# Batch 0's q of two head groups as whole rows, w_in in other pieces, four column pairs of the first batch by halves, transposes also on PSUM pairs, and a new hand-written order

## The chip, the cores and the metric

The kernel runs on one core of one Trainium2 chip. The metric is the time of one execution in device microseconds (us); the figure for a kernel is the median of its runs. The engines are called as the profile calls them: PE (matrix multiply, with PEld for the weight loads beside it), ACT and DVE (element by element), POOL and SP (here they mostly issue transfers).

## The reference, cut to what matters

```python
# q, k, v: (8 batches, 12 heads, 448 rows, 64); w_in: (768, 2048); w_out: (2048, 768)
scores = (q @ k.transpose) / 8
attn   = max(scores, 0)**2 / 448
x      = (attn @ v), heads side by side  -> (8*448 rows, 768)
h      = x @ w_in
out    = gelu_exact(h) @ w_out           # float32, 3584 x 768
```

There is no softmax, so the attention is: scores, relu, square, times v.

## The kernel before, in words

**Work of one batch.** A batch has three groups of four heads. First k and q are turned so that the 64 values of a head lie on partitions (`add_tk` L612 and `add_tq` L639 by PE for batches 0 and 1, tile `tp`, copied out to `kT` and `qT`; by DMA for later batches, `add_T_dma` L667). A step of `add_steps` (L734) multiplies a block of k with q into PSUM (tile `ps`, L752, array split into 64x64 parts), takes relu with the scale (tile `a_sq`; L769 on ACT or L771 on DVE) and squares it (L781 on DVE or L779 on ACT). `add_av` (L814) multiplies seven blocks of squares with v (tile `pav`, L831) and copies the result to `xT` (L519 on DVE, L521 on ACT). Batch 0's steps are done by halves of the 448 rows (`halves` L1468), so a step's q part is 224 wide. All other products use the whole 128x128 array: `x @ w_in` (plain: `add_f1` L880, tile `psh`, L891, gelu L901; or as 2x2 blocks with seven products instead of eight: `add_early` L989 and `add_unit` L1036, tile `pe`, L1048; for the last batch `add_block` L1188, tile `pb`, L1199) and `h @ w_out` (`add_group` L1339, tile `pso`, L1375, summed to `osb` by L1409, stored by L1328). The seven-product form needs sums of weights (`ws`, L962, and `t_sb`, L1309) and of activations (`t_x`, L1007, and `s_sb`, L1356), all on DVE.

**The beginning.** Batch 0's first head group is loaded by the ACT and SP queues as float32 (`k32`, `q32`) and cast by ACT and DVE (`early` L1528); everything else is loaded by POOL, cast on the way. Until data come, PE runs nine products of zeros (`spin`, L1510), and `Z` entries of the order put in further ones (`fill`, L1677). Batch 0's q is loaded by halves of its rows: `add_q(0, g, g + 1, 0, HC)` for groups 1 and 2, and one load `add_q(0, 0, G, HC, NC)` for the second half of all three groups. w_in comes in five pieces of columns of 128 (`WINS` L37, `add_win` L592, three DMAs each), w_out in five DMAs (`add_wout` L599). Six of batch 0's sixteen columns of `x @ w_in` are done plainly by halves of the rows (`HALF_M` L53: pairs starting at 0, 8, 10; 12 matmuls of 224 for a pair and half), columns 2 and 3 plainly for all rows (12 matmuls of 448), the rest by seven products.

**What sets the order.** A recorded list of operations is placed by `ORDER` (L83): each word is an engine (P and Q for PE, A for ACT, D for DVE, G for POOL, S for SP) and the number of an operation; `place` (L360) issues them in that order. Each engine's instructions run in that order, and an instruction that waits holds up all behind it on its engine. A `Q` calls the operation's `split` (L799 for steps, `add_av` has one too): the step then takes two single PSUM banks of `f_pp` (two in all) instead of one pair of banks of `w_pp` (three in all). The planner's durations in the tuples decide nothing at run time where `ORDER` names the operation, and `ORDER` names all.

Of the kernel before, what the change touches and what calls it, by code (L numbers as in the profile page):

```python
# [8 lines left out]
F32 = mybir.dt.float32  # L9
# [4 lines left out]
KC = 112  # L14
NC = S // KC
# [21 lines left out]
WINS = ((0, 2), (6, 8), (8, 12), (2, 6), (12, 16))  # L37
# [15 lines left out]
HALF_M = (0, 8, 10)  # L53
# [30 lines left out]
G0 G1616 G1 G3 G4 G7 D13 Z1024 A10 G118 A16 G2 P14 D15 P11 D12 P17 D18 P19 D20 P42 A43 P36 A37 P33  # L84
P21 D44 D22 P23 A24 D34 P51 P25 A52 D26 P48 Q39 D35 G117 P54 A49 D40 P63 A64 D55 P57 P27 D28 P29 D30
P69 P66 A58 D59 P31 D32 A70 D71 A67 G121 G6 G125 D38 P90 P93 D41 A94 D65 P131 A132 P102 A103 P129
P45 A46 A47 G126 Z672 A91 P84 D130 Q159 D50 D68 P72 G5 A160 D85 G8 G122 A73 G120 P111 A112 A53 D56
D74 P75 P133 D76 P156 D113 A157 A134 P81 D82 P139 A140 P60 D61 D83 P96 P108 D62 A97 D109 P137 P78
A79 D86 D80 P174 A175 D77 D92 P135 A136 D95 G124 P171 A172 D104 D98 P87 A88 P105 D89 A106 P168 A169
P141 A142 P162 D107 D110 D138 P195 A163 P99 D100 Q114 G119 P207 D101 D176 P165 A196 A115 D116 A158  # L90
P198 A199 D173 P143 A144 D208 D170 A166 D197 P240 A241 A161 D250 D251 P180 D181 D167 G128 G123 G9
D164 P222 A223 P192 P242 A243 P244 D253 D209 P145 A193 A146 P213 A214 A245 D194 P177 A178 D200 P189
A179 P183 D215 D190 D191 P246 A184 A247 P210 D182 A211 P216 P186 A187 D185 P248 A249 P258 P275 A217
D254 G127 G236 D188 P219 A276 G235 G238 G147 A220 Q201 D224 D212 D255 G148 P204 A202 A203 A205 D252
A221 P260 P277 A206 D259 P261 P278 A262 D409 D280 D218 D257 P265 D256 P282 A283 A266 Q225 A279 D412
D263 P270 P267 A226 A227 D371 D372 P284 D268 A269 P287 D285 P375 A264 A281 P392 A393 P273 G150 D271
P290 D288 P382 P399 D447 D374 A376 P378 P395 A274 D373 D450 A289 A291 D448 G151 P377 D451 P394 D397
A286 A400 A383 P387 P404 D380 A396 A379 P384 A272 D405 A406 P401 D388 P413 P430 A389 A414 A431 D385
A386 P420 P437 A421 D402 S228 A438 P407 D452 P390 D410 P416 A391 D411 P433 A408 D455 P442 S229 D454
A417 A434 P415 A398 G153 G154 P432 D443 A444 D435 A436 D418 P422 P439 A403 Q299 A300 P314 A315 P425  # L100
D423 P428 D456 D426 P459 A427 A424 D440 G234 A419 P311 P317 P445 P461 A441 D453 D449 D457 A318 D460
S230 S231 P463 P323 D312 A429 A381 A446 A313 D462 S232 P308 D316 S233 D301 A324 D309 D464 P350 P465
D466 A351 D352 P305 P302 A306 D310 P335 A307 P467 G237 G149 G152 G155 D458 D336 D468 A303 D304 P469
D470 P326 A327 P365 A366 P341 A342 D319 P471 P338 G239 G292 A339 A340 P320 D491 D472 A321 P332 A322
D337 D492 D343 G293 G294 D493 A333 P329 G295 D330 D367 S475 S476 P495 G296 A496 P497 P353 D498 P359
D334 D360 A331 A354 P362 A363 P499 S473 A500 P501 P356 P347 D325 A364 D328 P344 A357 A358 D355 D348
G297 D361 D345 D346 D349 G481 P511 A512 P520 A521 P503 P517 D502 A518 P526 P368 A369 D527 A519 P514
D504 S477 S478 G484 D494 S479 S480 P529 P505 D370 D583 P587 A513 P604 P507 D584 D515 G298 P594 A530
G487 A588 P589 A595 D605 D586 D522 A528 P607 P590 D508 D585 D592 P611 A516 P606 D608 A591 G482 G483
D621 D609 P599 A612 G485 G486 P596 S657 D531 P613 G488 D600 A601 S658 G489 S510 P623 P640 G663 D597  # L110
D614 P616 D617 A610 A641 A624 D622 P602 D506 P619 P625 P642 A593 A615 A603 A620 A598 Q523 D628 D645
A524 A646 P535 P626 P643 D525 S509 A536 A627 P630 P647 P538 A539 D631 D644 Q532 D533 A618 A534 P571
A572 P632 D648 P649 D673 P635 Q550 P553 A554 P652 D650 A651 D633 P638 P655 A656 D551 D674 A639 D636
A637 P677 P577 D653 A654 P559 A560 P547 S659 P679 D552 D675 P565 D548 S660 A678 D680 A578 A555 D540
P562 D563 D537 A566 S661 A567 D676 P681 P683 A682 D684 A634 P541 P574 P544 A545 D546 A629 A564 G666
P685 D686 S474 D542 D543 D693 D694 G490 P687 D688 S691 P689 D690 P568 A575 A549 A569 P556 D695 P719
A557 A558 A720 P713 D714 P697 D698 P725 A726 A727 A576 P728 D729 P722 D696 A570 P699 S692 D700 P731
P737 D732 P701 D702 D723 P703 P705 P746 D579 S662 G669 G664 G665 A561 D573 A747 P580 G667 A581 D704
D706 D730 D582 D785 P716 P709 A717 D710 S712 G668 G670 D786 P789 D788 G671 P806 A724 D790 P791 D794
D807 A738 P796 P813 D814 P707 A718 D787 A733 D715 P808 A739 D811 D708 A721 A812 P809 P792 D823 A810  # L120
P749 A750 Q734 D793 P740 A741 A795 D797 P798 P815 D816 P818 D819 D799 A742 A735 A736 D748 P825 P842
A843 P801 P821 P804 A751 A805 Q770 D802 P752 S711 A822 D826 P828 P845 A846 P832 D824 D753 D829 P849
D875 P827 S859 S860 S861 P844 D754 A850 P854 A800 S862 P834 P851 A771 A803 P879 D855 D830 D852 A833
D835 D847 P837 A817 A820 A853 P840 P857 P764 D876 D838 P755 D765 D877 A880 P883 A756 D878 A836 A858
A831 P773 A774 P761 D762 P881 D882 A841 G865 G868 A848 A884 P743 A763 A839 P767 D768 P918 D766 A775
P885 D886 P887 G672 D757 D888 A744 A856 A919 D745 P889 D890 D772 S893 P933 A934 D895 A935 P758 A759
D896 P779 A780 P776 A777 S863 A760 P891 P899 A900 S864 D898 P945 P927 D892 A778 P921 A922 A928 D946
D781 A947 P903 D920 P901 D897 P942 P948 A949 D769 D943 P782 A783 P924 G871 D902 A904 P930 D929 D931
D932 A925 P905 D906 A784 P907 D908 G866 P951 P915 D923 P939 D987 P909 G867 A940 D926 G869 G870 G872
D910 D988 P911 D912 S914 A952 P991 P1008 A916 A917 D990 Q963 D964 D944 P957 G873 A953 S1061 A958  # L130
D959 P936 A937 Q954 A938 P998 P1015 D992 P993 P1010 D1009 S1062 D989 A999 D950 P1011 A1016 A955
D1013 A1014 A956 P994 D996 P1003 D1012 A995 P1020 P1027 D1025 P1044 P1000 D1021 A1022 D1004 D1028
A1045 D1001 P1029 A997 P1046 D1049 A1050 D1032 A1005 P1030 P1047 D1026 P1017 D1018 A1031 P1034 P1051
D1048 S1063 S1064 S1065 A1002 P1023 P1036 P1053 D1052 D1054 A1035 D1037 P1039 P1056 P1006 G1067
A1007 G1070 D1057 D1079 A1024 P1042 P1059 A1060 P1081 D1040 S913 P978 A1041 A1043 A1058 P1117 D941
A979 P960 A961 D1077 D1078 D1118 P1150 D1151 S894 D962 P1120 P1083 A1121 P966 P972 A1082 P969 A973
P1085 P1141 D980 D967 D1084 A970 D1086 A968 D974 D1080 P981 A982 G874 A1055 P975 P1087 D1088 D1142
P1089 A1033 D1090 A976 P1091 A983 A1019 D1092 A1038 P1144 P1132 D1097 D977 P1147 A965 D971 A1133
A1148 D1134 P1093 P1101 D1094 S1095 S1066 P1129 A1130 P984 A1119 P1126 D1099 D1098 P1103 A985 A986
D1102 P1105 D1104 D1127 A1106 A1145 P1107 P1135 A1131 P1123 P1156 A1124 D1122 P1109 D1143 P1195  # L140
G1073 G1068 A1125 D1136 A1157 P1193 D1189 P1212 G1069 G1071 G1072 D1137 A1149 S1263 P1210 D1108
D1110 P1111 D1100 P1113 G1074 D1128 A1211 D1215 P1165 A1194 G1075 D1198 D1112 S1115 A1199 A1166
A1167 D1114 P1138 D1190 D1192 S1264 S1265 Q1153 S1096 P1200 P1217 P1196 P1213 A1139 A1154 D1140
# [262 lines left out]
def kernel(  # L406
# [169 lines left out]
    def add_v(b, g0, g1):  # L576
# [6 lines left out]
        for g in range(g0, g1):  # L583
            ld_v[b, g] = [o]
# [1130 lines left out]
```

## Time and profile before

| | |
|---|---|
| runs | 360.16, 361.66, 361.63 us; median 361.63 |
| profiled execution: span from first to last instruction | 358.5 us |
| what lies around the span, median less span | 3.1 us |
| PE, PEld busy | 350.0 us (98%), 248.0 us (69%) |
| DVE, ACT, POOL busy | 305.6 us (85%), 270.3 us (75%), 102.9 us (29%) |
| first transpose of PE | at 5.93 us |
| first plain product of `x @ w_in` (`psh`) | at 28.03 us |
| first product of the seven-product form (`pe`) | at 43.90 us |
| first product with w_out (`pso`) | at 71.57 us |
| last matmul ends | at 354.85 us |

Times within the profile are from the span's start. Matmuls overlap, so the busy time of PE counts some waiting as work; the distance between starts is the better measure, and the chain of waits and the timeline give it.

### The profile page before, as it was taken

Reading aid. Unit: us, or ns where it says so; the run is one execution under the profiler, and the core shown is the slowest. Engines: PE = TensorE matmul, PEld = TensorE weight load, DVE = VectorE, ACT = ScalarE, POOL = GpSimd, SP = SyncE. Lnnn points to the kernel's source line nnn. Section 1 sums busy time; section 2 is a strip of 40 time slices with the busy share of each in tenths; the row PEclk is TensorE's granted clock in tenths of the full one; section 3 lists DMA queues with packets and bytes.
Section 4 is the critical chain, followed back from the end, with each engine's and each line's share of the span. In section 5 each row is a group of like instructions: output and inputs, shape, how many; then the busy total and the mean of one; then the engine's idle time right before and its main releaser. Section 6 shows DMA issues by size and latency. Waiting matters only on the chain.

```text
span 358.5 us, 9223 instructions
## 1 busy us (share of the span) xinstructions
PE 350.0 (98%) x3841; PEld 248.0 (69%) x3841; DVE 305.6 (85%) x515; ACT 270.3 (75%) x437; POOL 102.9 (29%) x138
## 2 busy tenths in 40 slices
PE   8879999999999999999999999999999999999995
PEld 3557679955588655896557965579668855788663
DVE  2999999999997989988889898779988998595762
ACT  3999997899869896978978669789986778334300
POOL 8664816096193104700075100841000000000000
PEclk9999999999999999999999999999999999999999
DMA  9999999999999958995399941998402001012222
GB/s 171 197 201 204 201 204 157 146 145 148 183 141 146 214 84 127 154 169 79 63 90 159 214 69 51 88 171 209 72 3 90 2 0 46 3 44 90 88 87 91
DMA packets 124361, 43.01 MB, mean 120 GB/s; under 512 B 102688, under 2 KB 120992, under 8 KB 124320
## 3 DMA queue, kind: packets, MB, share of 16 engines
q0 software_dynamic: 85328, 22.47, 66.2%
q1 hardware_dynamic: 38448, 19.50, 26.0%
q8 instruction: 30, 0.49, 0.5%
q10 hardware_dynamic: 544, 0.46, 0.4%
q14 instruction: 11, 0.09, 0.1%
HBM read 45.61 MB, written 11.01 MB: 158 GB/s over the span
## 4 chain that ended last, share of the span: by engine, by line
PE 92%; ACT 5%; DVE 2%; issue 0%; DVEq 0%; ACTq 0%
PE pso L1375 37%; PE pe L1048 30%; PE ps L752 9%; PE pav L831 8%; PE pb L1199 4%; ACT a_sq L769 3%; PE psh L891 2%; PE spin L1510 1%; DVE a_sq L781 1%; DVE a_sq L771 1%; ACT xT L521 0%; PE tp L620 0%; PE fill L1677 0%; ACT a_sq L779 0%; ACT qT L521 0%
## 5 line engine op out<-in xcount | busy, mean ns | idle before, releaser
L769 ACT ACTIVATE a_sq<-ps 128x896 bf16<-128x896 f32 (+1 forms) x125 | 106.7, 893 | 14.5 <-PE ps L752 14.2
L781 DVE TENSOR_TENSOR a_sq<-a_sq 128x896 bf16<-128x896 bf16 (+1 forms) x108 | 63.8, 615 | 2.1 <-ACT a_sq L769 1.9
L1375 PEld LDWEIGHTS <-s_sb 128*128 128x128 bf16 x456 | 42.4, 98 | 32.3 <-issue 7.1
L1048 PEld LDWEIGHTS <-win_sb 128*128 128x128 bf16 x624 | 59.5, 98 | 2.7 <-issue 1.5
L771 DVE TENSOR_SCALAR a_sq<-ps 128x896 bf16<-128x896 f32 (+1 forms) x57 | 55.5, 988 | 2.6 <-PE ps L752 2.2
L779 ACT ACTIVATE a_sq<-a_sq 128x896 bf16<-128x896 bf16 x61 | 57.2, 959 | 0.5
L752 PE MATMUL ps<-qT,kT 64*64 64x448 bf16 (+1 forms) x756 | 49.7, 337 | 2.7 <-ACT a_sq L769 1.3
L1098 ACT ACTIVATE h_sb<-part 128x448 bf16<-128x448 f32 x78 | 43.2, 580 | 9.9 <-DVE part L1086 9.7
L1086 DVE TENSOR_TENSOR part<-pe,part 128x448 f32<-128x448 f32 x78 | 45.5, 620 | 5.3 <-PE pe L1048 3.6
L1375 PEld LDWEIGHTS <-h_sb 128*128 128x128 bf16 x336 | 31.9, 98 | 22.9 <-issue 4.0
L1048 PEld LDWEIGHTS <-ws 128*128 128x128 bf16 x468 | 44.1, 98 | 3.5 <-issue 2.9
L1375 PE MATMUL pso<-wout_sb,s_sb 128*128 128x384 bf16 (+2 forms) x232 | 41.1, 321 | 0.0
L1375 PE MATMUL pso<-t_sb,s_sb 128*128 128x384 bf16 x224 | 41.1, 327 | 0.0
L1375 PE MATMUL pso<-wout_sb,h_sb 128*128 128x384 bf16 x224 | 41.1, 327 | 0.0
L559 POOL DMA_DIRECT2D nk<-in_k_dram x36 | 34.7, 968 | 9.6 <-DMA wout_sb<-in_moe_w_out_dram 8.1
L831 PE MATMUL pav<-a_sq,v_sb 64*64 64x448 bf16 (+1 forms) x756 | 36.5, 329 | 0.8 <-DVE a_sq L781 0.8
L752 PEld LDWEIGHTS <-kT 64*64 64x64 bf16 x756 | 19.6, 105 | 23.7 <-issue 17.7
L1048 PE MATMUL pe<-t_x,win_sb 128*128 128x224 bf16 x312 | 34.5, 259 | 0.0
L1048 PE MATMUL pe<-xT,win_sb 128*128 128x224 bf16 x312 | 34.1, 259 | 0.0
L1048 PE MATMUL pe<-t_x,ws 128*128 128x224 bf16 x312 | 33.2, 259 | 0.0
L521 ACT COPY part<-pe 128x448 f32<-128x448 f32 x53 | 26.4, 541 | 8.9 <-PE pe L1048 6.2
L1409 DVE TENSOR_TENSOR osb<-pso,p_sb 128x384 f32<-128x384 f32 x42 | 23.3, 554 | 9.4 <-PE pso L1375 5.9
(74 smaller groups left out, 409.5 us busy)
## 6 DMA issues: line engine op xcount, KB each, us to landing
out_dram<-osb SPq DMA_DIRECT2D x19, 384.0 KB, 2.8
nq<-in_q_dram POOLq DMA_DIRECT2D x38, 112.0 KB, 5.8
nk<-in_k_dram POOLq DMA_DIRECT2D x36, 112.0 KB, 5.8
v_sb<-in_v_dram POOLq DMA_DIRECT2D x5, 672.0 KB, 7.6
v_sb<-in_v_dram POOLq DMA_DIRECT2D x9, 224.0 KB, 8.0
win_sb<-in_moe_w_in_dram POOLq DMA_DIRECT2D x8, 192.0 KB, 9.2
wout_sb<-in_moe_w_out_dram POOLq DMA_DIRECT2D x4, 384.0 KB, 12.7
wout_sb<-in_moe_w_out_dram POOLq DMA_DIRECT2D x1, 1536.0 KB, 15.8
```

The costliest lines, as they stand in the source:

```text
L521: A.copy(dst, src)
L559: nc.gpsimd.dma_start(nk[b][:, g0, :, e], rows[:, e].rearrange("p (i d) -> p i d", d=D))
L752: nc.tensor.matmul(side(ps, e)[64 * j : 64 * j + 64, x * w : x * w + w], kT[r, g, i * 128 + 64 * j : i * 128 + 64 * j + 64], moving, start ...
L769: A.activation(to, x, AF.Relu, scale=c_att)
L771: V.tensor_scalar(to, x, c_att, 0.0, op0=mybir.AluOpType.mult, op1=mybir.AluOpType.max,)
L779: A.activation(ar, ar, AF.Square)
L781: V.tensor_mul(ar, ar, ar)
L831: nc.tensor.matmul(side(pav[0], e)[o2 : o2 + 64, :w], vt[b][r, 2 * g + e, bass.ts(i, D)], box["a2"][r, e, o : o + w], start=(i == 0), stop ...
L1048: nc.tensor.matmul(bank[name][:, y, z * HS : z * HS + HS], w[:, k, bass.ts(mm, 128)], right()[:, k], start=first and k == 0 and z == 0, st ...
L1086: V.tensor_add(get(to), ps(name), get(other))
L1098: A.activation(h_ring()[:, m : m + 2, o + half[c].start : o + half[c].stop], src().rearrange("p (x n) -> p x n", x=2), AF.Gelu,)
L1375: nc.tensor.matmul(box[bank][:, n0:n1], left()[:, kf], right()[:, kf, n0:n1], start=bool(need) and kf == 0, stop=kf == K2 - 1, skip_group_ ...
```

## The change

Loads and pieces: `WINS` becomes (0,2), (8,12), (2,6), (12,16), (6,8). Groups 1 and 2 of batch 0's q are each loaded whole; of the second half of the rows only group 0 remains. The identity matrix that the transposes need is made on POOL ahead of the first load instead of behind it. `HALF_M` gets a fourth pair, 2, and columns 2 and 3 are no longer done for all rows at once; the products are the same in total, as 24 matmuls of 224 instead of 12 of 448. The transposes of `add_tk` and `add_tq` may take a pair of banks of `w_pp` instead of a bank of `f_pp` where the order says `Q`. `add_unit` waits for the pieces of w_in that it reads. `ORDER` is wholly new: all engines' instructions stand in another order, and some copies, relus and squares are on the other of ACT and DVE. The durations in the planner's tuples are changed in many places; since `ORDER` names every operation they move nothing by themselves. The core of the diff:

```diff
-WINS = ((0, 2), (6, 8), (8, 12), (2, 6), (12, 16))
+WINS = ((0, 2), (8, 12), (2, 6), (12, 16), (6, 8))
-HALF_M = (0, 8, 10)
+HALF_M = (0, 8, 10, 2)
 ORDER = """
-G0 G1616 G1 G3 G4 G7 D13 Z1024 A10 G118 A16 G2 P14 D15 P11 D12 P17 D18 P19 D20 P42 A43 P36 A37 P33
+G2 D16 Q17 D18 A13 Q14 A19 P20 D21 G3 P22 D23 A15 P39 A40 P36 D37 P42 G4 Z672 P24 D25 D38 A41 A43
...
+    def t_bank(wide):
+        if wide:
+            return w_pp.tile([128, 2, 2 * NB], BF16, tag="w", name="tp")[:, 0]
+        return f_pp.tile([128, 2 * NB], BF16, tag="f", name="tp")
+
+    def widen(op, ev, wide):
+        def split():
+            wide.append(True)
+            op.need, ev.frees = ("w",), ("w",)
+        op.split, op.alt = split, "w"
+        op.after = ident_op
...
-            tp = f_pp.tile([128, n], BF16, tag="f", name="tp")
+            tp = t_bank(wide)[:, :n]
...
-            tp = f_pp.tile([128, 2, n], BF16, tag="f", name="tp")
+            tp = t_bank(wide)[:, : 2 * n].rearrange("p (j n) -> p j n", j=2)
...
-    PLAIN += [(m, None) for m in (2, 3)]
...
+        ld = list(dict.fromkeys(ld_win[m + r] for m in ms for r in (0, M1)))
-        p1 = product("b", plain(0, 0), x(0, 0), xs, True)
+        p1 = product("b", plain(0, 0), x(0, 0), xs + ld, True)
...
     for g in (1, 2):
         add_k(0, g, g + 1)
-        add_q(0, g, g + 1, 0, HC)
+        add_q(0, g, g + 1)
         add_v(0, g - 1, g)
     add_v(0, 2, 3)
-    add_q(0, 0, G, HC, NC)
+    add_q(0, 0, 1, HC, NC)
...
-    for m in (2, 3):
-        add_f1(0, m, bias=F1B_BIAS)
```

Three places of the order follow, the kernel before first, then the changed one; lines are those of each file. ACT, the twelve rows up to its first gelu (`h_sb<-psh`), before:

```order
L521 CAST xT<-pav 128x224
L769 ACTIVATE a_sq<-ps 128x2x224
L779 ACTIVATE a_sq<-a_sq 128x896
L769 ACTIVATE a_sq<-ps 128x896
L521 COPY kT<-tp 128x896
L521 COPY qT<-tp 128x896
L769 ACTIVATE a_sq<-ps 128x896 x3
L521 COPY qT<-tp 128x896
L769 ACTIVATE a_sq<-ps 128x896
L521 CAST xT<-pav 128x224
L769 ACTIVATE a_sq<-ps 128x896 x2
L901 ACTIVATE h_sb<-psh 128x2x224
```

ACT in the changed kernel, from its first relu (`a_sq<-ps`) to its first gelu:

```order
L796 ACTIVATE a_sq<-ps 128x896 x2
L796 ACTIVATE a_sq<-ps 128x2x224
L796 ACTIVATE a_sq<-ps 128x896
L796 ACTIVATE a_sq<-ps 128x448 x2
L796 ACTIVATE a_sq<-ps 128x896 x3
L796 ACTIVATE a_sq<-ps 128x2x224
L796 ACTIVATE a_sq<-ps 128x896 x2
L523 CAST xT<-pav 128x224 x4
L796 ACTIVATE a_sq<-ps 128x896 x2
L523 CAST xT<-pav 128x224
L796 ACTIVATE a_sq<-ps 128x896 x2
L930 ACTIVATE h_sb<-psh 128x2x224
```

What moved: before the first gelu ACT now has 12 whole and 4 half relus and 5 small copies; all copies of batch 1's transposes, and squares, stand behind it or on DVE (in the kernel before ACT runs 17 whole and 4 half relus, 5 copies of transposes, a square and 4 small copies up to there).

POOL, the loads after the first one, before (k, q and v of batches 0 and 1; `128x3x256` is the first piece of w_in):

```order
L472 DMA nq<-in_q_dram 112x4x128
L556 DMA nk<-in_k_dram 128x2x448
L472 DMA nq<-in_q_dram 112x4x128
L472 DMA nq<-in_q_dram 112x12x128
L472 DMA nq<-in_q_dram 112x4x256
L579 DMA v_sb<-in_v_dram 128x2x448
L556 DMA nk<-in_k_dram 128x2x448 x2
L579 DMA v_sb<-in_v_dram 128x2x448
L556 DMA nk<-in_k_dram 128x2x448
L472 DMA nq<-in_q_dram 112x4x256
L579 DMA v_sb<-in_v_dram 128x2x448
L492 DMA win_sb<-in_moe_w_in_dram 128x3x256
```

POOL in the changed kernel, from the identity matrix to the second piece of w_in (columns 8 to 11):

```order
L1527 AFFINE_SELECT ident<-ident 128x128
L558 DMA nk<-in_k_dram 128x2x448
L474 DMA nq<-in_q_dram 112x4x256 x2
L558 DMA nk<-in_k_dram 128x2x448
L474 DMA nq<-in_q_dram 112x4x128
L581 DMA v_sb<-in_v_dram 128x2x448 x3
L474 DMA nq<-in_q_dram 112x4x256
L494 DMA win_sb<-in_moe_w_in_dram 128x3x256
L495 DMA win_sb<-in_moe_w_in_dram 64x3x256
L496 DMA win_sb<-in_moe_w_in_dram 64x3x256
L494 DMA win_sb<-in_moe_w_in_dram 128x3x512
L495 DMA win_sb<-in_moe_w_in_dram 64x3x512
```

What moved: the two pieces of w_in stand right behind batch 0 and one load of batch 1. In the kernel before, five loads of batch 1 stand ahead of the first piece and one more ahead of the second.

SP at the end of the program, before:

```order
L675 DMA_TRANSPOSE qT<-nq 128x8x112
L1328 DMA out_dram<-osb 128x768 x10
L1328 DMA out_dram<-osb 128x384 x3
L1328 DMA out_dram<-osb 128x256
L1328 DMA out_dram<-osb 128x128
```

SP in the changed kernel:

```order
L697 DMA_TRANSPOSE kT<-nk 128x7x128
L1358 DMA out_dram<-osb 128x768 x8
L1358 DMA out_dram<-osb 128x384 x3
L1358 DMA out_dram<-osb 128x128
L1358 DMA out_dram<-osb 128x256
```

What moved: the two last stores, and the two DVE sums ahead of them, have changed places. In both kernels PE makes the 128 columns first and the 256 columns last.

More of the change, by code (lines that the diff above doesn't have):

```diff
@@ L844, in add_av @@
         op = sch.add(
-            (("PE", d, d + 0.24),), fn, deps, mode="A", bias=bias + AV_BIAS, need=("w",),
+            (("PE", d, d + 0.18),), fn, deps, mode="A", bias=bias + AV_BIAS, need=("w",),
             frees=("a",) * gone,
         )
+        op.after = [o for (bb, gg, hh), o in AV.items() if bb == b and hh == half and half is not None]
         AV[b, g, half] = op
@@ L964, in one @@
                 ),
-                deps,
+                deps, after=sch.fills,
             )
@@ L1162, in xsum @@
             return sch.add(
[L1163 removed]
+                (("DVE", 0.415, 0.535),),
                 lambda e: V.tensor_tensor(t(n)(), l(), r(), op=op), deps + xs + gone,
+                after=[o for oo in gates.values() for o in oo],
             )
@@ L1511, with add_fill, fn @@
     ctx.enter_context(tc.manual_schedule())
+    def add_fill(n):
+        def fn(e):
+            fill = f_pp.tile([128, NB], F32, tag="f", name="fill")
+            zeros = zero[:D, :1].to_broadcast([D, NB])
+            for x in range(0, n, NB):
+                c = min(NB, n - x)
+                nc.tensor.matmul(
+                    fill[:D, :c], zero[:D, :D], zeros[:, :c], start=True, stop=True
+                )
+        return sch.add((("PE", n / 2400, n / 2400),), fn, need=("f",), frees=("f",), mode="A")
+    sch.fills += [add_fill(int(x[1:])) for x in ORDER.split() if x[0] == "Z"]
+    ident_op.append(sch.add((("POOL", 0.31, 0.4),), lambda e: make_ident()))
     for g in (1, 2):
         add_k(0, g, g + 1)
-        add_q(0, g, g + 1, 0, HC)
+        add_q(0, g, g + 1)
         add_v(0, g - 1, g)
     add_v(0, 2, 3)
-    add_q(0, 0, G, HC, NC)
+    add_q(0, 0, 1, HC, NC)
     add_win(0)
@@ L1541 @@
     ld_k[0, 0] = []
-    for eng, i0, i1, t in (("DVE", 0, K_CUT, 5.1), ("ACT", K_CUT, NK, 5.45)):
+    for eng, i0, i1, t in (("DVE", 0, K_CUT, 4.55), ("ACT", K_CUT, NK, 5.04)):
         c = slice(i0 * D, i1 * D)
@@ L1669 @@
         pe_q.append(o)
-    def add_fill(n):
-        def fn(e):
-            fill = f_pp.tile([128, NB], F32, tag="f", name="fill")
-            zeros = zero[:D, :1].to_broadcast([D, NB])
-            for x in range(0, n, NB):
-                c = min(NB, n - x)
-                nc.tensor.matmul(
-                    fill[:D, :c], zero[:D, :D], zeros[:, :c], start=True, stop=True
-                )
-        return sch.add((("PE", n / 2400, n / 2400),), fn, need=("f",), frees=("f",), mode="A")
-    sch.fills = [add_fill(int(x[1:])) for x in ORDER.split() if x[0] == "Z"]
-    sch.add((("POOL", 0.31, 0.4),), lambda e: make_ident())
-    add_vgate(B - 1)
     sch.run({"PE": pe_q, "POOL": pool_q})
```

257 lines of the change are left out of this document (135 added, 122 removed).

## The prediction

> **What bounds the kernel now.** I read the page first, then the chain of waits, then a table by stage, then ACT's timeline in the first stage.
>
> ```profile
> span 358.5 us, 9223 instructions
> PE 350.0 (98%) x3841; PEld 248.0 (69%) x3841; DVE 305.6 (85%) x515; ACT 270.3 (75%) x437; POOL 102.9 (29%) x138
> ```
>
> PE is the bound, yet 98% hides waits, since matmuls overlap. The chain of waits (start, length, what) gives what a run of matmuls costs from start to start:
>
> ```profile
> 93.06 1.32 PE pav L831 x28
> 94.39 0.38 PE ps L752 x8
> 94.77 1.41 PE pso L1375 x8
> 96.17 0.50 PE ps L752 x8
> ...
> 98.38 1.41 PE pso L1375 x8
> 99.79 1.15 PE pe L1048 x12
> 100.94 1.14 PE pso L1375 x7
> ```
>
> Twelve `pe` cost 1.15, so 0.096 each (`psh` and `pb` the same). Seven `pso` cost 1.14, 0.163 each. Four whole `ps` cost 0.19, 28 `pav` 1.32, halves half of that. Eight `pso` behind `pe` would cost 1.30 but behind `ps` they cost 1.41; eight `ps` cost 0.38 behind `pav` and 0.50 behind `pso`. So **a change between the 64x64 and the 128x128 form costs 0.115**.
>
> With 0.03 for a transpose (180 of them, 5.4) all PE work comes to 326.6: `pso` 127.4, `pe` 104.6, `pb` 16.1, `psh` 9.2, `ps` and `pav` 63.9. The order of before has 135 changes of form, 15.5 us. The rest of the clock I call **lag**: clock, less work done, less changes of form done. By stage (length, then busy time of PE, PEld, DVE, ACT, POOL, granted clock, DMA):
>
> ```profile
> 0.00:5.93 5.93, 4.94 (x12) 1.34 (x13) 0.62 (x4) 2.52 (x4) 4.80 (x11) 1.00 0.77 172
> 5.93:28.03 22.10, 18.31 (x483) 12.78 (x482) 21.08 (x40) 19.99 (x30) 14.81 (x22) 1.00 1.36 195
> 28.03:43.90 15.87, 15.80 (x229) 11.46 (x226) 15.16 (x29) 15.12 (x24) 10.65 (x14) 1.00 1.29 202
> 43.90:71.57 27.67, 27.67 (x320) 25.26 (x318) 27.21 (x43) 23.96 (x48) 7.99 (x10) 1.00 1.71 171
> 71.57:354.85 283.28, 283.28 (x2808) 197.19 (x2806) 240.87 (x401) 208.76 (x334) 64.61 (x83) 1.00 0.81 104
> ```
>
> At 28.03, the first `psh`, PE has done 13.0 of work (5.4 transposes, 4.9 `ps`, 2.7 `pav`) and 27 changes (3.1): lag 11.9. At 43.90, the first `pe`, 27.5 and 35 changes (4.0): lag 12.4. At the last matmul it is 12.4 still (354.6 less 342.2). So **all that PE waits is lost before 44 us, nearly all of it before 28**; later only work and changes of form count. In 5.93 to 28.03 DVE and ACT are the full engines. ACT's timeline there:
>
> ```profile
> 8.04 1.35 ACT L769 ACTIVATE a_sq<-ps 128x448 bf16<-128x448 f32 x2 [2.27 <-PE ps L752]
> 9.27 0.91 ACT L521 COPY kT<-tp 128x896 bf16<-128x896 bf16 x1
> 10.06 5.81 ACT L769 ACTIVATE a_sq<-ps 128x896 bf16<-128x896 f32 x7
> 15.65 1.02 ACT L521 COPY qT<-tp 128x896 bf16<-128x896 bf16 x1
> ...
> 17.24 0.74 ACT L521 CAST xT<-pav 128x224 bf16<-128x224 f32 x2
> 17.70 1.97 ACT L769 ACTIVATE a_sq<-ps 128x896 bf16<-128x896 f32 x3
> ...
> 29.39 0.58 ACT L901 ACTIVATE h_sb<-psh 128x448 bf16<-128x448 f32 x1
> ```
>
> From start to start a whole relu takes 0.80 (seven in 5.59), a turned copy 0.79, a half relu 0.43 (1.23 less 0.80), a small `xT` copy 0.23. Up to the first gelu ACT has 17 whole relus, 4 half ones, 5 turned copies, a square (0.84) and 4 small copies: 21.0, where the timeline has 21.35. So ACT sets the 28.03, without a gap.
>
> **The change part by part.**
>
> *ACT before the first `psh`.* Now 12 whole relus, 4 half, 5 small copies: 9.6 + 1.7 + 1.15 = 12.5. Batch 1's copies and the square are moved behind or to DVE. The first relu: PE's transposes wait for the fills.
>
> ```profile
> 0.99 4.02 PE L1510 MATMUL spin<-zero 128*128 128x512 bf16 x9 [0.99 <-DVE zero L1493]
> 4.94 1.06 PE L1677 MATMUL fill<-zero 64*64 64x512 bf16 x2
> 5.93 0.44 PE L620 MATMUL tp<-ident,nk 128*64 128x128 bf16 x8
> ...
> 16.72 0.44 PE L1677 MATMUL fill<-zero 64*64 64x512 bf16 x2
> ```
>
> The two fills of 4.94 now come later, so the transposes can start at 5.0, and the first relu at 7.25 instead of 8.04 (other end: 8.04, since group 1's k, issued 0.3 later, stands ahead of the first step; I take the earlier, the nearest row being the 0.9 of the fills). First gelu then at 19.7 and the first `psh` 1.36 before it (29.39 less 28.03), at 18.4. The order has 8.4 of work (106 transposes, 136 half `ps`, 84 half `pav`) and 16 changes (1.8) ahead of it: **lag 8.2** instead of 11.9. The same sum at each later gelu gives 8.2 at the second, 8.1 at the fourth, 8.0 at the seventh, 6.6 at the first `pe` (31 whole relus): ACT asks for no more than 8.2 later.
>
> *w_in.* The second `psh` needs columns 8 to 11 by 20.4. POOL's issues wait for earlier landings, and so show their pace (in brackets the wait and its cause):
>
> ```profile
> 3.84 2.41 POOL L472 DMA_DIRECT2D nq<-in_q_dram  x3
> ...
> 12.71 0.74 POOL L492 DMA_DIRECT2D win_sb<-in_moe_w_in_dram  x1 [0.45 <-DMA nq<-in_q_dram]
> ...
> 21.21 0.77 POOL L492 DMA_DIRECT2D win_sb<-in_moe_w_in_dram  x1 [0.89 <-DMA v_sb<-in_v_dram]
> ```
>
> ```profile
> nq<-in_q_dram POOLq DMA_DIRECT2D x1, 336.0 KB, 6.7
> ...
> nq<-in_q_dram POOLq DMA_DIRECT2D x2, 112.0 KB, 4.4
> ```
>
> Between those two waits seven loads of 224 KB land: 1.21 each. The half rows issued at 3.84 land near 8.3, the 336 KB of half rows issued at 4.56 at 11.3: 3 us for 1.5 loads, 1.9 a load. Whole rows at 1.21 would bring the same bytes by 10.1. Then 4 loads and 1152 KB of w_in follow, 9.14 loads by size, 11.1 us: columns 8 to 11 at 21.2 (at 22.3 if whole rows gain nothing). PE waits 0.9 for them, and ACT behind it: lag 9.1.
>
> [...]
>
> *Behind it.* From the first `psh` to the first `pe` 20.5 of work and 20 changes follow; before lost 0.5 there, I add 0.4. **Lag 9.5** in place of 12.4: 2.9 less. Ends: 8.2 (no wait) and 11.0 (relu at 8.04 and 22.3).
>
> *Changes of form.* The new order has 124 instead of 135: 11 x 0.115 = 1.3 less. Ends: 1.1 and 1.5.
>
> *Tail.* PE ends alike. Then:
>
> ```profile
> 354.89 0.62 DVE L1409 TENSOR_TENSOR osb<-pso,osb 128x256 f32<-128x256 f32 x2 [0.76 <-PE pso L1375]
> 355.34 0.81 SPq L1328 DMA_DIRECT2D out_dram<-osb  x2
> ```
>
> DVE now does the 128 columns while PE works on the 256, and one store instead of two is issued behind the last sum (0.4 earlier): 0.3 less, between 0.2 and 0.4.
>
> *At no price.* 12 more weight loads: PEld is 69% busy. 24 matmuls of 224 for 12 of 448: the same columns, 0.03. Transposes in wide banks: the copy is the same; where a step had to wait for such a bank it would wait for one copy (0.4 to 0.8), and before the first step none does. Elementwise work that changes engine:
>
> ```profile
> L781 DVE TENSOR_TENSOR a_sq<-a_sq 128x896 bf16<-128x896 bf16 x106 | 63.0, 620 | 1.9 <-ACT a_sq L769 1.7
> L779 ACT ACTIVATE a_sq<-a_sq 128x896 bf16<-128x896 bf16 x61 | 57.2, 959 | 0.5
> ```
>
> DVE has 111 squares, ACT 56; with the copies DVE gains about 4 us and ACT loses 7, so DVE goes from 85 to 87%. PE's waits hide it except before 72, where DVE is full (27.21 of 27.67). There its sum up to the first `osb` add is 65.3 by its own start-to-start times, against 66.8 before; it arrives 1.5 earlier where PE wants it 2.9 earlier. In before PE had no wait there; two runs of `ps` and `pso` (2 us) stand between that add and the next product that needs its bank, so I leave it at nothing; other end 1.5.
>
> **Sum.** 2.9 + 1.3 + 0.3 = 4.5 from the profiled span: 358.5 to 354.0. The median lies 3.1 above the span, so 361.6 becomes **357.1**.
>
> **The rivals.**
>
> *Whole rows gain nothing:* lag 10.6, time 358.2. For: the 336 KB load may only have shared the DMA engines with other queues. Against: the 1.9 a load.
>
> *DVE takes over as the bound before the first `pso`:* its sum is shorter by 1.5 only, and the last w_out pieces now stand behind eight loads of batch 2. Gain 4.5 less up to 2: 359.1. Against: DVE was as full there in before, and PE had no wait.
>
> [...]
>
> *Slower:* columns 8 to 11 land as late as before. PE stands in order at the second `psh`, nothing behind it can run, and from 20.4 each us of delay is a us of lag.
>
> ```profile
> 19.70 0.63 POOL L494 DMA_DIRECT2D win_sb<-in_moe_w_in_dram  x1 [0.59 <-DMA nq<-in_q_dram]
> ```
>
> ```profile
> DMA to landing us min/median/max: 7.7/8.6/10.9
> ```
>
> The last of their three DMAs was issued at 19.70 and by the median of w_in's DMAs landed 8.6 later, at 28.3. Work and changes up to the second `psh` are 12.2, so lag would be 16.1: with the 0.4 behind it 4.1 more than before, less the 1.6 of changes and tail, time 364.1. It turns slower than before from a landing at 25.8. For: DMAs of several loads share the engines and land late together. Against: five loads that stood ahead now stand behind.
>
> *It does not do what it says:* waits come back at places that I did not sum, near 361.
>
> **How the numbers follow.** Chances: forecast 0.55 (own range by the ends above, 355.5 to 358.9), whole rows 0.12, DVE 0.12, clock 0.05, late w_in 0.09, waits elsewhere 0.07. The first four are faster by over 0.5% (under 359.8; 0.5% is about what a measurement of this kernel can tell from no change), but for a part of DVE's: 0.79. Within 0.5%: 0.10. Slower (over 363.4): 0.11, the late w_in and a part of the last. The range goes from 354.8 (lag 8.2 with the better ends is 355.5, less half the 1.5 by which the three runs differ) to 360.4, and leaves out the slower case and half of the waits elsewhere.
>
> **What would show it.** First `psh` near 18.4 (17.5 to 19.5), second near 21.3, first `pe` near 42.3; lag at `pe` about 9.5 and unchanged at the end; no fills before the first transpose near 5.0; last two DVE sums apart, not in a row. If the first `psh` is right but lag at the end is over 11, waits have come back behind it; if the second `psh` starts after 24, the landing was wrong; if the first relu is at 8 or later, the start was.

## The result, and the profile after

The changed kernel takes **421.9 us** (418.7 to 423.0), the kernel before 360.9 us beside it: a ratio of 1.168, with a 95% interval of 1.163 to 1.173. The forecast was 357.1 us. The page of the changed kernel, its engines and its granted clock in 40 slices of 10.5 us:

```profile
span 421.1 us, 9250 instructions
PE 368.1 (87%) x3853; PEld 255.8 (61%) x3853; DVE 312.2 (74%) x523; ACT 266.7 (63%) x429; POOL 102.6 (24%) x138
...
PEclk9999988969999999987999999999999899999999
```

This execution took 423.0 us. The work is the same, yet PE is busy for 87% only, and up to the last matmul the granted clock falls to 0.50 in five places, where the kernel before has 1.00 in every stage up to there. By stage (length, then busy time of PE, PEld, DVE, ACT, POOL, granted clock, DMA; cut at the first transpose, the first `psh`, `pe` and `pso`, and the last matmul's end):

```profile
0.00:5.45 5.45, 4.03 (x11) 1.20 (x11) 0.67 (x4) 1.80 (x3) 4.53 (x11) 1.00 0.65 162
5.45:19.66 14.21, 12.70 (x331) 9.39 (x331) 12.53 (x25) 12.65 (x23) 9.99 (x15) 1.00 1.35 196
19.66:44.12 24.46, 23.17 (x422) 17.27 (x419) 22.71 (x43) 22.66 (x35) 16.24 (x21) 1.00 1.30 202
44.12:90.53 46.41, 34.59 (x308) 27.53 (x305) 29.67 (x47) 24.48 (x49) 21.28 (x27) 0.87 1.60 154
90.53:417.82 327.29, 293.65 (x2796) 200.37 (x2792) 246.22 (x406) 205.10 (x323) 50.59 (x66) 0.98 0.61 83
```

Up to the first `pe`, at 44.12 instead of the 42.3 forecast, the miss is under 2 us. From there on PE idles 12 us of 46 and then 34 of 327. The same in lag (clock, less work done, less 0.115 per change of form, by the starts in the traces), for kernels of this study too:

| | median us | first `psh` at | lag there | at first `pe` | at first `pso` | at first `pb` | at the last matmul |
|---|---|---|---|---|---|---|---|
| before | 360.9 | 28.0 | 11.9 | 12.4 | 12.4 | 12.5 | 12.6 |
| predicted | 357.1 | 18.4 | 8.2 | 9.5 | 9.5 | 9.5 | 9.5 |
| changed | 421.9 | 19.7 | 9.4 | 11.1 | 30.0 | 69.9 | 76.8 |
| e1, changed, words by plan | 382.3 | 20.1 | 9.9 | 11.2 | 15.4 | 32.1 | 36.2 |
| e4, changed, best words | 376.5 | 22.0 | 11.8 | 12.5 | 15.5 | 28.7 | 31.5 |
| e3, before, words against | 456.7 | 28.7 | 12.6 | 13.8 | 37.7 | 110.4 | 110.5 |
| e5, changed, single banks | 365.9 | 19.6 | 9.4 | 10.7 | 11.3 | 21.0 | 21.6 |
| e5, before, single banks | 363.6 | 29.2 | 13.1 | 14.0 | 14.1 | 16.0 | 16.1 |
| e9, all edits | 359.2 | 19.8 | 9.6 | 10.5 | 11.1 | 12.3 | 12.3 |

So the prologue brought 1.3 of the 2.9 forecast, and then 65.7 us were lost behind it. The four largest waits of PE in the changed kernel (what waits, for what; us in all, times, longest):

```profile
PE pe L1076 <- DVE part L1114: 20.6, 21, 3.0
PE pe L1076 <- DVE part L521: 11.3, 12, 2.6
PE pe L1076 <- ACT part L523: 8.2, 13, 1.0
PE pb L1229 <- DVE part L1266: 3.3, 6, 0.7
```

All of them are products of the seven-product form waiting for the copies and sums (`part`) that empty their banks. They are 43.4 us. In five stretches, 23.9 us in all, the granted clock was 0.50; PE was busy for 21.3 of them, which costs up to 10.7. With the 45.5 us that PE stands idle by the table of stages this makes 56 of the 65.7; the rest is not taken apart here. Now one such place, the first two pairs of units. PE, then ACT, then DVE (start, length, what, idle before it and its releaser):

```profile
44.12 1.32 PE L1076 MATMUL pe<-xT,win_sb 128*128 128x224 bf16 x12
45.28 1.31 PE L1076 MATMUL pe<-t_x,ws 128*128 128x224 bf16 x12
46.78 1.31 PE L1076 MATMUL pe<-t_x,ws 128*128 128x224 bf16 x12 [0.19 <-DVE part L521]
...
53.22 0.75 PE L1076 MATMUL pe<-xT,ws 128*128 128x224 bf16 x6
55.29 0.73 PE L1076 MATMUL pe<-t_x,win_sb 128*128 128x224 bf16 x6 [1.32 <-DVE part L1114]
57.31 1.08 PE L1076 MATMUL pe<-t_x,win_sb 128*128 128x224 bf16 x6 [1.29 <-DVE part L1114]
```

```profile
45.52 0.55 ACT L523 COPY part<-pe 128x448 f32<-128x448 f32 x1
...
56.06 0.54 ACT L1126 ACTIVATE h_sb<-pe 128x448 bf16<-128x448 f32 x1 [0.75 <-PE pe L1076]
```

```profile
46.10 0.63 DVE L521 COPY part<-pe 128x448 f32<-128x448 f32 x1 [1.23 <-ACT part L523]
...
54.08 1.16 DVE L1114 TENSOR_TENSOR part<-pe,part 128x448 f32<-128x448 f32 x2 [0.92 <-PE pe L1076]
56.63 1.16 DVE L1114 TENSOR_TENSOR part<-pe,part 128x448 f32<-128x448 f32 x2 [1.40 <-ACT h_sb L1126]
```

The first DVE row is the odd one. The copy at 46.10 empties the first unit's bank, whose six matmuls were issued by 44.7. DVE has nothing else to do for 1.23 us and starts when ACT ends its copy of the **other** unit's bank, at 46.07. No value passes between the two copies. The built program shows the same (engine's row, then the engines whose semaphores it waits for; the numbers are the tiles'):

```
ACT  COPY part_1169<-pe_1156 128x448 [waits DVE, PE]
DVE  COPY part_1194<-pe_1156 128x448 [waits Activation]
```

Both read the tile `pe_1156`, of two banks, one bank for each of a pair of units (`add_unit`, `y` 0 and 1). ACT's copy has the earlier place in the sequence in which the program records its operations, so DVE's copy waits for it; it doesn't wait for PE at all. At 56.63 it is the same: a sum of one unit waits for a gelu (56.06) that reads the other's bank, and PE's product at 57.31 waits for that sum. From 52 to 57.3 PE, DVE, ACT, DVE and PE take turns.

### The profile page after: what moved, and what is told of

Its sections match the earlier page's. It is cut to its first block, busy times and chain, and to the rows that moved or that the text cites. A ratio compares the mean times of both kernels' runs of the same rounds, so it can differ in the third digit from the quotient of the medians.

```text
span 421.1 us, 9250 instructions
## 1 busy us (share of the span) xinstructions
PE 368.1 (87%) x3853; PEld 255.8 (61%) x3853; DVE 312.2 (74%) x523; ACT 266.7 (63%) x429; POOL 102.6 (24%) x138
## 4 chain that ended last, share of the span: by engine, by line
PE 70%; DVE 14%; ACT 11%; issue 3%; DMA 1%; POOL 0%; DVEq 0%; ACTq 0%
PE pso L1405 30%; PE pe L1076 20%; PE ps L779 7%; PE pav L858 7%; DVE part L1114 5%; ACT a_sq L796 5%; PE pb L1229 3%; ACT part L523 3%; DVE part L521 2%; ACT h_sb L1126 2%; PE psh L920 2%; DVE part L1266 2%; DMA nk<-in_k_dram 1%; DVE ws L991 1%; ACT a_sq L806 1%
## 5 line engine op out<-in xcount | busy, mean ns | idle before, releaser
L796 ACT ACTIVATE a_sq<-ps 128x896 bf16<-128x896 f32 (+1 forms) x137 | 110.8, 861 | 19.0 <-PE ps L779 18.7
L1076 PEld LDWEIGHTS <-win_sb 128*128 128x128 bf16 x624 | 62.0, 101 | 36.5 <-issue 33.5
L1076 PEld LDWEIGHTS <-ws 128*128 128x128 bf16 x468 | 46.9, 103 | 21.7 <-issue 18.9
L1126 ACT ACTIVATE h_sb<-part 128x448 bf16<-128x448 f32 x78 | 43.1, 577 | 21.6 <-DVE part L1114 21.6
L806 ACT ACTIVATE a_sq<-a_sq 128x896 bf16<-128x896 bf16 x56 | 51.8, 951 | 0.5
L1076 PE MATMUL pe<-xT,win_sb 128*128 128x224 bf16 x312 | 38.5, 272 | 14.2 <-DVE part L1114 7.5
L1076 PE MATMUL pe<-t_x,win_sb 128*128 128x224 bf16 x312 | 39.2, 268 | 13.0 <-DVE part L1114 10.2
L798 DVE TENSOR_SCALAR a_sq<-ps 128x896 bf16<-128x896 f32 (+1 forms) x45 | 46.6, 1044 | 4.1 <-PE ps L779 4.0
L1076 PE MATMUL pe<-t_x,ws 128*128 128x224 bf16 x312 | 38.1, 272 | 8.2 <-DVE part L521 4.8
L479 POOL DMA_DIRECT2D nq<-in_q_dram x36 | 29.9, 835 | 10.4 <-DMA wout_sb<-in_moe_w_out_dram 8.1
L521 DVE COPY part<-pe 128x448 f32<-128x448 f32 x28 | 17.2, 622 | 20.0 <-ACT part L523 11.5
```

What stands on the lines that cost most here:

```text
L796: A.activation(to, x, AF.Relu, scale=c_att)
L798: V.tensor_scalar(to, x, c_att, 0.0, op0=mybir.AluOpType.mult, op1=mybir.AluOpType.max,)
L806: A.activation(ar, ar, AF.Square)
L1076: nc.tensor.matmul(bank[name][:, y, z * HS : z * HS + HS], w[:, k, bass.ts(mm, 128)], right()[:, k], start=first and k == 0 and z == 0, st ...
L1126: A.activation(h_ring()[:, m : m + 2, o + half[c].start : o + half[c].stop], src().rearrange("p (x n) -> p x n", x=2), AF.Gelu,)
```

## The theories

**A, the pair tile.** An access to a `pe` or `pb` tile waits for every access of that tile that another engine has recorded before it, in whichever bank. Which of two has to wait isn't set by the engines' orders but by the sequence of the words of `ORDER` across engines, which a listing of each engine's own order doesn't show. In the built program PE's products wait at 31 places for an access of the other bank only in the kernel before, and at 77 in the changed one. The count alone is not the cost: the runs e1 and e3 below have 68 and 36 such places and lose 22 and 97 us, since ACT and DVE wait for each other in the same way and since a wait costs only where the other access is late.

To put numbers on it I replayed the built programs: each engine in its order, durations and landings from the two traces, waits as recorded. The last matmul then starts at 355.0 for before (the trace has 354.6) and at 408 for changed (417.5; the replay knows no half clock). With the waits between different banks left out, changed comes to 352.8. These are estimates from the traces' durations.

**B, engine order.** The new order is too tight in itself: DVE does six squares in a row (48.80 to 52) ahead of the sums that PE needs. **C, clock.** PE runs slow and the waits follow from that.

## The experiments

**e1: other words, same engine orders.** The words of the changed kernel's table, sorted by the start that its planner gives them. At the first pair:

```diff
-P261 P278 A279 A219 D253 D254 D257 D258 P268 P285 D262
+D258 P261 A208 A225 P278 D262 D256 P268 A279 D259 A219 P285
```

> The changed kernel with the words of its table written in another sequence: sorted by the start that its own planner gives each word. Every engine issues exactly the same instructions in the same order as in the changed kernel; only the sequence in which the program records them differs, and with it which of two accesses of one PSUM tile by different engines has to wait for the other. Theory A (pair tile): one product tile `pe` or `pb` holds two units in its two banks, and an access by one engine waits for every access of the tile that another engine has recorded before it, also when that touched the other bank; the waits of PE behind 44 us come from there. Then the time falls a long way: a replay of all instructions with the durations of the two traces and these waits ends the last matmul at 375.5 (for the changed kernel as given it says 408, where the trace has 417.5), so about 381 us. Theory B (engine order): the new order of the instructions on the engines is too tight in itself (squares and sums ahead of what PE waits for): 418 to 424, as the changed kernel. Theory C (clock): waits are a result of a lower TensorE clock: 418 to 424 as well.

Measured: 382.3 us, 1.060 of before (1.057 to 1.064). **40 us are gone with no engine's instruction moved.** C falls: with four largest waits of 14.0 us instead of 43.4 the granted clock is 1.00 up to the last matmul, so the half clock was a result of the waits. B falls as the cause of these 40. What PE still waits for in e1:

```profile
PE pe L1076 <- ACT part L523: 5.0, 9, 1.1
PE pe L1076 <- DVE part L1114: 4.9, 11, 0.9
PE pe L1076 <- DVE part L521: 2.3, 5, 0.7
PE pb L1229 <- DVE part L1266: 1.8, 4, 0.7
```

**e2: the same for before.**

> The kernel before with the words of its table sorted by its planner's start in the same way; again every engine's instructions are the same in the same order. Theory A: in the kernel before hardly any access waits for one of the other bank, so nothing is to be had: replay 355.9 for the last matmul against 355.0, so 361 to 363 us. Theories B and C: 360 to 362.

Measured: 361.0 us, 1.001 (0.9997 to 1.003): the same. Sorting by itself brings nothing where PE loses no time to the other bank. This also answers a rival of e1: the sequence of words settles which buffer a tile gets too (in e1, e2 and e3 many tiles of `a_sq`, `part` and PSUM lie in other buffers than without the edit, in e3 against what its expectation says). In e2 that moves nothing, nor does it in e9.

**e3: the fault put into the kernel before.** 58 exchanges; the first stretch reads:

```diff
-P219 A276 G235 G238 G147 A220 Q201 D224 D212 D255 G148 P204 A202 A203 A205 D252 A221 P260 P277 A206 D259
+P219 G235 G238 G147 Q201 D224 D212 D255 G148 P204 D252 D259 A276 A220 A202 A203 A205 A221 P260 P277 A206
```

> The kernel before, with 58 pairs of words exchanged in the sequence of its table: in each, two accesses of one `pe` tile by different engines, of different banks, are recorded the other way round. No engine's instructions change, nor their order, nor any buffer. Theory A: the waits appear in the old order too; the replay puts the last matmul at 431.8 instead of 355.0, so about 438 us (430 to 450 if the clock falls too). Theory B: the engine order is that of before, so 360 to 362. Theory C: 360 to 362.

Measured: 456.7 us, 1.265 (1.258 to 1.272), more than the changed kernel loses. The size is above the replay's 438, and above the 450 that was allowed for a lower clock. The granted clock is 0.944 in the mean, 0.50 for 51 us in all, which can cost up to 26 us; that this is the whole of the difference is not shown. The first pair of units, on ACT and then on PE; in before PE runs the same sequence without a gap, the second `pe` at 46.98:

```profile
49.44 0.53 ACT L521 COPY part<-pe 128x448 f32<-128x448 f32 x1 [2.34 <-DVE part L519]
49.86 0.92 ACT L769 ACTIVATE a_sq<-ps 128x896 bf16<-128x896 f32 x1
```

```profile
45.31 1.31 PE L1048 MATMUL pe<-xT,win_sb 128*128 128x224 bf16 x12
46.56 0.38 PE L752 MATMUL ps<-qT,kT 64*64 64x448 bf16 x4
46.77 1.49 PE L831 MATMUL pav<-a_sq,v_sb 64*64 64x448 bf16 x28
48.09 0.36 PE L752 MATMUL ps<-qT,kT 64*64 64x448 bf16 x4
50.84 2.40 PE L1048 MATMUL pe<-xT,win_sb 128*128 128x224 bf16 x12 [2.39 <-ACT a_sq L769]
```

The copy on ACT (`A276`) now waits 2.34 for DVE's copy of the other bank (`D259`, until 49.40), a relu stands behind it, and PE waits for that relu: its row names only the last link.

**e4: the best words for the changed engine order**, shown here against e1:

```diff
-D258 P261 A208 A225 P278 D262 D256 P268 A279 D259 A219 P285
+P261 A208 A225 P278 P268 D262 P285 D256 A279 D259 A219
```

> The changed kernel once more with the same instructions in the same order on every engine, its words in the sequence that a search over the replay found best (35,000 sequences of the accesses of each `pe` and `pb` tile tried). Theory A: last matmul 369.6 by the replay, about 375.5 us; the replay with no waits between different banks at all ends at 352.8, so some 16 us of them are left whatever the sequence, and the time does not come down to the 357.1 that was predicted. Theory B and C: 418 to 424.

Measured: 376.5 us, 1.043 (1.039 to 1.048). As theory A has it, part of the loss stays: the new engine order lets a product of one unit follow the emptying of the other so closely that with a shared tile one of the two has to wait. That no sequence avoids this is the replay's word, by the 35,000 sequences tried, and not shown by a run.

**e5: single banks.** The pair is two tiles, so that nothing is ordered across banks:

```diff
-    w_pp = pool("w_pp", 3, PS)
+    w_pp = pool("w_pp", 6, PS)
-                    bank[name] = w_pp.tile([128, 2, NB], F32, tag="w", name="pe")
+                    bank[name] = [w_pp.tile([128, NB], F32, tag="w", name="pe") for _ in range(2)]
-                            bank[name][:, y, z * HS : z * HS + HS],
+                            bank[name][y][:, z * HS : z * HS + HS],
```

and the same for `pb`, `ps`, `pav`, `tp` and `spin`. A step's relu then is two instructions instead of one.

> The changed kernel as given, table and all, but its three PSUM tiles of two banks are six tiles of one bank, taken two at a time; a product tile `pe` or `pb` is then two tiles, one for each unit, and no access waits for one of another bank. Price: the relu of a step reads two tiles and so is two instructions of 448 columns instead of one of 896. Theory A (pair tile): all waits of PE behind 44 us go; the replay puts the last matmul at 354.6 (408 with pairs), so about 360 us (358.5 to 361.5), the same as before within 0.5%. Theory D: what was left with the best sequence of words (376.5 us) is the engine order itself, whatever the tiles: 374 to 379, or more by the doubled relus.

> The kernel before with the same edit of its PSUM tiles: the price of the doubled relus without anything to be won. Theory A: nothing waited there for another bank; replay 357.2 instead of 355.0 for the last matmul, so about 362.5 us. The changed kernel with single banks minus this one is what the change is worth when the tiles do not hide it: by the replay 2.6 us less, by the recorded sum 4.5 less. Theory D: the same, 362 to 363.

Measured: changed 365.9 us (362.5 to 367.8), 1.013 (1.010 to 1.017); before 363.6 us, 1.008 (1.007 to 1.010). No wait of `pe` or `pb` is left in the changed kernel; theory D, that the engine order itself keeps the rest of the loss, is wrong. The largest wait of PE is now another:

```profile
PE ps L779 <- DMA qT<-nq: 5.4, 1, 5.4
```

But 360 was expected, and the lag shows a new loss of 9 us between 80 and 120 us (in an execution of 367.8 us, the longest of the six). PE in that stretch, then its stages (columns as above):

```profile
91.42 1.49 PE L858 MATMUL pav<-a_sq,v_sb 64*64 64x448 bf16 x28
98.30 0.96 PE L779 MATMUL ps<-qT,kT 64*64 64x448 bf16 x8 [5.39 <-DMA qT<-nq]
99.19 2.74 PE L1405 MATMUL pso<-wout_sb,s_sb 128*128 128x384 bf16 x8
```

```profile
90.00:98.30 8.30, 2.92 (x43) 1.43 (x42) 5.54 (x10) 3.86 (x7) 0.01 (x1) 0.94 1.78 130
98.30:104.10 5.80, 5.80 (x24) 2.45 (x24) 0.56 (x1) 2.68 (x5) 2.80 (x6) 0.50 1.02 201
```

PE waits 5.39 for the turned q of batch 3, and for the next 5.8 us it runs at half clock: eight `pso` take 2.5 from start to start instead of 1.3. The waits on SP's queue and SP itself in the same run say why:

```profile
SPq L1366 <- DVE osb L1439: 12.7, 1, 12.7
```

```profile
71.62 1.22 SPq L697 DMA_TRANSPOSE qT<-nq  x1
85.61 0.82 SPq L1366 DMA_DIRECT2D out_dram<-osb  x2
86.60 1.63 SPq L697 DMA_TRANSPOSE kT<-nk  x1
88.33 2.36 SPq L697 DMA_TRANSPOSE qT<-nq  x1
```

SP reaches an output store at 72.9 and stands there until its sum is done; batch 3's transposes queue behind it. In the kernel before two of them stand ahead of that store and start at 81.98 and 83.84. In e5 the first turned q of batch 3 lands at 98.17.

**e6 and e7: two terms of the prologue**, both on top of e5.

```diff
+                for c in (0, HC):
+                    part = nq[b][:, 4 * g0 : 4 * g1, c * D : (c + HC) * D]
+                    nc.gpsimd.dma_start(part, q_view(b, g0, g1, c, c + HC))
```

> The changed kernel with single banks, but the q of head groups 1 and 2 of batch 0 is loaded by two transfers of half rows each (512 bytes a piece) instead of one of whole rows (1024 bytes). If whole rows bring what the recorded sum took (1.2 against 1.9 a load), the first half of group 0 lands near 12.5 instead of 11.1, columns 8 to 11 of w_in near 23.5 instead of 22.3, and the time is about 1 us more than with whole rows. If they gain nothing, landings and time stay within 0.3 us.

Measured: 361.8 us. From the landing of k, the load ahead of them, to the last of the q of groups 1 and 2 it takes 2.35 us in e5 (two whole loads, 1.20 and 1.15 apart) and 2.46 in e6 (four halves, 0.53 to 0.65 apart): **half rows cost 0.1 us for the two loads, not the 0.7 for each that the forecast took** (1.9 less 1.2). The landings moved all the same, nearly as the first case of the expectation has it: group 0's half lands at 11.49 instead of 10.31, columns 8 to 11 at 23.06 instead of 22.06, and the first `psh` starts at 20.18 instead of 19.63. Of these 1.2 us, 0.55 are there before any q lands (k at 6.74 instead of 6.19), and 0.54 come at the load behind the halves, which has two more issues of 0.7 ahead of it on POOL. That the whole is 4 us faster than e5 is not from the rows: the store holds SP as long here, but the turned q lands at 95.44, PE waits 1.85 for it instead of 5.39, and no half clock follows (granted clock 1.00 in the mean). How late q is thus differs from run to run.

```diff
-G2 D16 Q17 D18 A13 Q14 A19 P20 D21 G3
+G3 G2 D16 Q17 D18 A13 Q14 A19 P20 D21
```

> The changed kernel with single banks, its load of group 1's k issued ahead of the making of the identity matrix instead of behind it, as the first thing on that queue. If the late first relu (7.99 in the changed kernel, 7.25 in the recorded sum) comes from that order, k lands 0.3 to 1.0 earlier than 6.99, the first relu starts near 7.3 and the first `psh` is as much earlier; the second `psh` still waits for columns 8 to 11 of w_in, which land no earlier, so the time falls by 0 to 0.6 us. If the landing is set by the loads that share the engines with it, nothing moves.

Measured: 365.0 us, the interval overlaps that of e5. k lands at 6.30 (6.19 in e5), the first relu starts at 7.28 (7.31), the first `psh` at 19.60 (19.63): nothing moves, so the order of the two is not what makes k late in the changed kernel. There it lands at 6.99 and the first relu starts at 7.99; in e1 and e4, which have pair tiles too, k lands at 7.50 and 7.57, in the five runs with single banks at 6.2 to 6.7. The cause stays open.

**e8: the transposes ahead of the store**, on top of e7; on SP:

```diff
+L697 DMA_TRANSPOSE kT<-nk 128x7x128
+L697 DMA_TRANSPOSE qT<-nq 128x8x112
 L1366 DMA out_dram<-osb 112x768
 L1366 DMA out_dram<-osb 16x768
-L697 DMA_TRANSPOSE kT<-nk 128x7x128
-L697 DMA_TRANSPOSE qT<-nq 128x8x112
```

> The kernel of the run before (changed kernel, single banks, group 1's k issued first), with one more edit on SP's queue: the first two transposes of batch 3 stand ahead of the first output store instead of behind it, as in the kernel before. Theory A2: with the waits between banks gone, what is left between 80 and 120 us is a wait of PE for the transposed q of batch 3, because SP stands at that store for 12.7 us (until its sum is there at 85.6) with the transposes queued behind it; and the idle time makes the clock fall to half for some us more. Then the first of these transposes is issued near 83 instead of 87, PE's wait near 95 goes or falls under 1 us, the lag at 120 us is near 12 instead of 18, and the time about 359 us (358 to 361) instead of 365. Rival: the transposes are late because of their loads and the shared DMA engines; then they land as late as before and the time stays at 363 to 366.

Measured: **359.6 us**, 0.998 of before (0.996 to 0.9996), 5.5 less than e7 and 2.2 less than e6, where q happened to be less late. On SP now:

```profile
82.55 1.26 SPq L697 DMA_TRANSPOSE kT<-nk  x1
84.19 1.38 SPq L697 DMA_TRANSPOSE qT<-nq  x1
85.69 0.98 SPq L1366 DMA_DIRECT2D out_dram<-osb  x2
```

The first turned q of batch 3 lands at 91.61, the lag at 120 us is 12.0, and behind 44 us PE's waits are 0.6 us in all.

**e9: e8 with the words by plan.**

> The same kernel, its words sorted by the planner's start. With single banks the sequence of words should hardly matter any more: the replay gives 353.6 for the last matmul against 354.1, so the time is within 1 us of the other's. If the sequence still matters by more, an access of another kind is ordered by it as well.

Measured: 359.2 us, 0.9975 of before (0.996 to 0.999): the sequence matters no more once each bank is its own tile. e9 beats both kernels, if only by 0.25%. Its engines, to be held against the first page:

```profile
span 357.0 us, 9430 instructions
PE 350.2 (98%) x3853; PEld 251.3 (70%) x3853; DVE 311.3 (87%) x564; ACT 269.8 (76%) x544; POOL 102.4 (29%) x138
```

## Why the prediction was wrong

The step that failed is "**all that PE waits is lost before 44 us**; later only work and changes of form count". This was read from the trace of before, where it holds, and carried over to a kernel whose every engine order is new. 65.7 us of lag came behind the first `pe`; the prediction's own sign for it, a lag over 11 at the end, reads 76.8. The runs showed two mechanisms in its place: waits across the banks of a pair tile (e1, e3, e5), with the half clock that came with them in both kernels (0.50 for 23.9 us in the changed one, for 51 in e3); and, hidden behind them, SP's store ahead of batch 3's transposes (e5, e8). The rival "waits come back at places that I did not sum" was right in kind, but near 361 and with 7%; no mechanism was sought for it.

The terms one by one:

- *First `psh` at 18.4:* it came at 19.66. The first relu was at 7.99, the other end named, since k landed at 6.99; another 0.5 passed between relu and `psh`. The relu at 7.25 came nearly so in e5, e7 and e8 (7.3), not in e9 and e6 (7.5 and 7.7) nor in e1 and e4 (8.5 and 8.6).
- *w_in, columns 8 to 11 at 21.2:* they landed at 22.32, which is the rival's 22.3. Whole rows did come at 1.2 and 1.1 a load, as forecast, but by e6 half rows cost next to nothing more (2.46 us against 2.35 for the two loads). The price of 1.9 a load (3 us for 1.5 loads is rather 2.0) was mis-sized: the 3 us of that load were not the row's length.

```profile
19.66 1.23 PE L920 MATMUL psh<-xT,win_sb 128*128 128x224 bf16 x11
21.82 0.27 PE L920 MATMUL psh<-xT,win_sb 128*128 128x224 bf16 x1 [0.94 <-issue]
22.02 0.77 PE L779 MATMUL ps<-qT,kT 64*64 64x224 bf16 x24
22.72 1.51 PE L920 MATMUL psh<-xT,win_sb 128*128 128x224 bf16 x14
```

- *Second `psh` near 21.3:* 22.72, right behind a run of `ps` and 0.4 after the landing, so the landing is not what it waited for last. The first one's last matmul stands 0.94 on nothing that the profile shows ("issue"); the same matmul does so in e1, e4, e5, e6, e7 and e9, by 0.2 to 0.7, and not in e8. Its cause stays open.
- *Lag at the first `pe` 9.5:* 11.1. The sign held, the gain is 1.3 instead of 2.9.
- *Changes of form, 1.3:* in e9 80 of them pass between the first `pso` and the first `pb`, and the lag, which charges 0.115 for each, grows by 1.2 there, waits included. So one costs 0.115 to 0.13.
- *Tail, 0.3:* wrong, if by little. From the last matmul's end to the span's end it takes 3.3 us instead of 3.6, as forecast, but PE does not end alike: it stands 0.40 ahead of its last eight matmuls for the sum of the 128 columns, which now comes ahead of them. From the start of the 128 columns to the span's end it is 5.35 us in the changed kernel and 5.09 in before.

```profile
416.79 1.03 PE L1405 MATMUL pso<-wout_sb,s_sb 128*128 128x256 bf16 x8 [0.40 <-DVE osb L1439]
```

- *What lies around the span, 3.1:* mis-sized. The span of 358.5 is that of the execution of 360.16 (in later runs a time of 360.16 has a span of 358.4, one of 361.66 a span of 359.9), and the median 361.63 is another's. In every run here the time less the span of the same execution is 1.7 to 2.1, in the changed kernel 1.9. By the forecast span of 354.0 the time would have been 355.9.
- *Elementwise work and wide transposes at no price:* right in e9, where PE stands idle for 0.4 us in all behind 44 us. In the changed kernel copies on ACT and DVE are where the waits sit, but by their tile, not by their load: DVE is 74% busy. Its busy time grew by 6.6 us and ACT's fell by 3.6, where 4 and 7 were forecast.
- *Rivals:* the slower one (w_in late, 364.1) did not happen. DVE as the bound before the first `pso` did not either, by e9's lag of 11.1 there. The 0.05 for the clock was the author's estimate; what the runs show is a granted 0.50 early on in e4 (6.8 us from 8.5) and e8 (3.4 us from 14.5), so in some executions, and in the changed kernel 1.00 in both stages from 5.45 to 44.12.

On the same tiles, e9 against before with single banks, the edits and the change together are worth 363.63 less 359.16, 4.5 us. That this is the forecast sum is partly luck: e9 has the SP edit, its lag grows by 1.8 behind the first `pe`, and its tail brings nothing, while single banks cost the kernel before 3.5 us.

## What to carry to other kernels

When a change replaces a whole order, the trace of before bounds only what the order keeps: walk the bounding engine's waits in the new program, with the trace's durations, before any lag is carried forward. A listing by engine hides one thing that decides such waits: the sequence in which accesses of one tile by different engines are recorded. Two units that share a tile of several banks are tied by it; give each bank its own tile. Another sequence can help without that, but e4, the best that was found, still took 376.5 us. And look at each in-order queue for a store that waits and has loads behind it: in e5 it held SP's for 12.7 us.

## What the runs showed of the hardware

- The order across banks is the program's, not the chip's: with a tile for each bank PE, ACT and DVE worked on the two banks of a pair, and of the 43.4 us that PE waits at `pe` and `pb` in the four largest waits of the changed kernel none is in e5's list of waits.
- Idle time cost twice in e5: after 5.39 us of waiting PE ran 5.8 us at a granted clock of 0.50. In the changed kernel a granted clock of 0.50 came in stretches of 3.4 and 6.8 us, 23.9 in all, although no wait of PE was over 3.0 there. In the 5 us ahead of each of the five stretches, at a granted 1.00, PE was busy for 2.0 to 2.7 us.
